# First stage of batches 2 to 7: all 32 columns through the folded transform, from a re-laid-out copy of x

## The chip, the cores and the metric

One NeuronCore of one Trainium2 chip runs the whole program. The metric is device time in microseconds of one execution, the median of several runs; the traces are of one profiled execution.

## What is computed

The program mixes tokens with a global filter in the frequency domain and then applies a two-layer network with SiLU, all in fp32. Cut to what matters:

```
x: 8 x 3008 x 256,  filt_r, filt_i: 1505 x 256,  w_in: 256 x 2048,  w_out: 2048 x 256
y   = irfft(rfft(x, axis=1) * (filt_r + 1j*filt_i), n=3008, axis=1)
h   = y.reshape(24064, 256) @ w_in
out = (h * sigmoid(h)) @ w_out
```

## The kernel before

**The transform.** A sequence of 3008 is split as 94 rows times 32 columns. Stage 1 takes, for each column, a transform over the 94 rows; `forward` takes the transform over the 32 columns; then come the filter's products, `inverse`, and `stage3`, which makes `y`. Between the stages the data goes through DRAM (`d1`, `d2`) to change its layout. Eight batches are treated one after the other.

Stage 1 of batches 2 to 7 uses the symmetry of the cosine and sine tables twice. Rows n and n + 47 are added and subtracted. For columns 0 to 23 (three pieces f = 0, 1, 2 of 8 columns) row n is also paired with its mirror row, which leaves 24 rows to sum over. A folded piece is loaded into `x_all` by `load_fold` (L400), combined on VectorE by `fold` (L412) in four parts k = 0 to 3, multiplied by `stage1_fold` (L427) in sixteen 24-row by 32-column matmuls with 512 columns of data (four column pairs q, each in a quarter of the rows and with a PSUM bank of its own, times four tables k), copied out of PSUM by `evict_fold` (L438), and stored to `d1` from GpSimd's queue (L446). The mirrored rows are prepared in DRAM by `reverse_x` (L388), which copies x in reversed row order. Columns 24 to 31 (pieces u = 6, 7 of 4 columns) are not mirrored: `load_x` (L311) loads them, `sums` (L332) forms sum and difference, `stage1` (L339, matmuls at L354) multiplies with 47 rows and 64 table columns, and `evict_t1` (L381) and L361 copy out.

**The network.** The tokens of a batch are treated in 6 groups (`pairs`), each in 8 steps over the hidden width, so 48 steps per batch (`STEPS`). A step is seven matmuls of `hidden` (L745) and seven of `project` (L804), interleaved in eight rounds; both use a seven-product scheme with 2 x 2 blocks, so VectorE must form sums of PSUM results and of SiLU outputs (helper `combine`, L729) between them. `project` lags `hidden` by one step. Within a step `hidden` writes two PSUM tiles, px (bank "x") and pyz (bank "yz"), each with a single buffer: px is read by ScalarE (copies at L766, L773, L779 and a SiLU at L762), pyz by VectorE. The first pyz matmul of a step waits for the VectorE sum that reads the last pyz of the step before.

**The order.** Nothing is scheduled automatically; each engine executes its instructions in the order in which they are recorded. `put(step, round, piece)` (L619) enters a piece of the spectral work, `until` (L1200) records everything that is due between the rounds. `plan` (L625) enters a batch's pieces at steps relative to `at`, the batch's first step; "step -44" means `at - 44`. `open_step` (L684) enters pieces ahead of a step, after the first two matmuls of `project`; such pieces may use the banks "x" and "yz" (`HIDDEN`, L617) while `hidden` has not yet begun the step. In step -44 the unfolded pieces u = 6 (in the hidden banks) and u = 7 (in the two buffers "f") stand so (L649). Loads and stores of the output are issued from SyncE's queue (SP) in the same order; output tiles are transposed on VectorE (L871) and stored at L882, two of these transposes in step -46 and two in step -45.

For batch 2 the trace has step -46 at 412.21 us, step -45 at 418.25 us and step -44 at 424.30 us, counted from the start of the span.

The functions that the diff touches:

Of the kernel before, what the change touches and what calls it, by code (L numbers as in the profile page):

```python
# [46 lines left out]
FP32 = mybir.dt.float32  # L47
# [23 lines left out]


# [23 lines left out]
def dft_tables():  # L96

    wf = np.zeros((128, 2, 64))
    for par in range(2):
        for i, idx in enumerate(ORDER):  # L100
            ph = 2 * np.pi * (np.arange(N1) * (2 * idx + par) % 94) / 94
            for h in range(2):
                wf[64 * h:64 * h + N1, par, 2 * i] = np.cos(ph)
                wf[64 * h:64 * h + N1, par, 2 * i + 1] = -np.sin(ph)


# [58 lines left out]
    return (wf.astype(f32), wx.reshape(96, 128).astype(f32), wq.astype(f32), wi.astype(f32),  # L165
# [5 lines left out]
def kernel(  # L171
    ctx: ExitStack,
    tc: tile.TileContext,
    x: bass.AP,
    filt_r: bass.AP,
# [8 lines left out]
    wf_host, wx_host, wq_host, wi_host, d_host, e_host = dft_tables()  # L184
    wf_dram = nc.inline_tensor(wf_host, name="wf_tbl")
# [34 lines left out]
    wf_t = cpool.tile([128, 2, 64], FP32)  # L220
# [47 lines left out]
    def spectral(b):  # L268
# [42 lines left out]
        def load_x(u, queue=None):  # L311


            xs[u] = x_t[u % 2]
            if b == 1:
                xs[u] = xs[u].rearrange("p a n -> p (a n)")
                return load_rows(xs[u], u, 1, queue)
            for h in range(2):
                for r0, nr in ((0, 32), (32, N1 - 32)):
                    nc.sync.dma_start(  # L320
                        out=xs[u][64 * h + r0:64 * h + r0 + nr],
                        in_=bass.AP(tensor=x.tensor,
                                    offset=x.offset + (b * S + 32 * r0 + 4 * u + 2 * h) * C,
                                    ap=[[32 * C, nr], [32 * N1 * C, 2], [1, 2 * C]]))
# [7 lines left out]
        def sums(u):  # L332
            ut = x_t[0] if u == 7 else upool.tile([128, 2, 512], FP32, name=f"u_{b}_{u}", tag="u")
            xt = xs.pop(u)
            for par, op in ((0, ALU.add), (1, ALU.subtract)):
                nc.vector.tensor_tensor(out=ut[0:111, par], in0=xt[0:111, 0], in1=xt[0:111, 1], op=op)
            us[u] = ut

        def stage1(u, ahead=True):  # L339
            t1 = tpool.tile([128, 2, 2, C], FP32, name=f"t1_{b}_{u}", tag="t")  # L340
            ps = [bank(b, f"pa_{b}_{u}_{h}", HIDDEN[h] if b > 1 and u == 6 else None) for h in range(2)]
            if b == 1:
                xt = xs.pop(u)
                for h in range(2):
                    nc.tensor.matmul(out=ps[h].rearrange("p n c -> p (n c)"), lhsT=wx_t,  # L345
                                     rhs=xt[0:96, 512 * h:512 * h + 512], start=True, stop=True)
                if ahead and u + 2 < 8:
                    load_x(u + 2)
            else:
                ut = us.pop(u)  # L350
                for par in range(2):
                    for h in range(2):
                        rows = slice(64 * h, 64 * h + N1)
                        nc.tensor.matmul(out=ps[h][64 * par:64 * par + 64], lhsT=wf_t[rows, par],  # L354
                                         rhs=ut[rows, par], start=True, stop=True)
            if b > 1 and u == 7:
                us["t1"] = t1, ps
                return
            for h in range(2):
                copy = nc.scalar.copy if b == 1 or h == 0 else nc.vector.tensor_copy  # L360
                copy(out=t1[:, h], in_=ps[h])  # L361
            if b == 1:
                us["t1", u] = t1
                if ahead:
                    store_rows(u)
                return
            store_t1(u, t1)
# [7 lines left out]
        def store_t1(u, t1):  # L375
            for par in range(2):
                nc.gpsimd.dma_start(
                    out=d1[par].rearrange("s p n c -> (s p) n c")[:, 4 * u:4 * u + 4, :],
                    in_=t1[64 * par:64 * par + 2 * NS].rearrange("p h n c -> p (h n) c"))

        def evict_t1(u, h):  # L381
            t1, ps = us["t1"]
            copy = nc.vector.tensor_copy if h else nc.scalar.copy
            copy(out=t1[:, h], in_=ps[h])
            if h:
                store_t1(u, t1)

        def reverse_x():  # L388

            us["xr"] = dpool.tile([2, 24, 32 * C], FP32, name=f"xr_{b}", tag="xr")  # L390
            at = x.offset + b * S * C
            nc.sync.dma_start(out=us["xr"][:, 1:24],
                              in_=bass.AP(tensor=x.tensor, offset=at + 46 * 32 * C,
                                          ap=[[32 * N1 * C, 2], [-32 * C, 23], [1, 32 * C]]))
            for k in range(2):
                nc.sync.dma_start(out=us["xr"][k, 0:1],
                                  in_=bass.AP(tensor=x.tensor, offset=at + (1 - k) * 32 * N1 * C,
                                              ap=[[32 * C, 1], [1, 32 * C]]))

        def load_fold(f):  # L400

            at = x.offset + (b * S + 8 * f) * C
            for q in range(4):
                rows = slice(32 * q, 32 * q + 24)
                n0 = (8 * f + 2 * q) * C
                nc.sync.dma_start(out=x_all[rows, 0],
                                  in_=bass.AP(tensor=x.tensor, offset=at + 2 * q * C,
                                              ap=[[32 * C, 24], [32 * N1 * C, 2], [1, 2 * C]]))
                nc.sync.dma_start(out=x_all[rows, 1],
                                  in_=us["xr"][:, :, n0:n0 + 2 * C].rearrange("k m n -> m k n"))  # L410
# [16 lines left out]
        def stage1_fold(f):  # L427
            ut = us.pop("f")
            rhs = x_all[:, 0, 0], x_all[:, 1, 0], ut[:, 0], ut[:, 1]
            ps = [bank(b, f"pf_{b}_{f}_{q}", (0, 1, None, None)[q]) for q in range(4)]  # L430
            for k in range(4):
                for q in range(4):
                    rows = slice(32 * q, 32 * q + 24)
                    nc.tensor.matmul(out=ps[q][32 * k:32 * k + 32], lhsT=wq_t[rows, k], rhs=rhs[k][rows],  # L434
                                     start=True, stop=True)
            us["ps"] = ps

        def evict_fold(f, q):  # L438
            if q % 2 == 0:
                us["tf"] = tpool.tile([128, 2, 2, C], FP32, name=f"tf_{b}_{f}_{q}", tag="t")  # L440
            copy = nc.scalar.copy if q < 2 else nc.vector.tensor_copy
            copy(out=us["tf"][:, q % 2], in_=us["ps"][q])  # L442
            if q % 2:
                n0 = 8 * f + 2 * q - 2
                for k in range(4):
                    nc.gpsimd.dma_start(  # L446
                        out=d1[k // 2, :, k % 2, n0:n0 + 4],
                        in_=us["tf"][32 * k:32 * k + NS].rearrange("p q n c -> p (q n) c"))
# [161 lines left out]
        return dict(us=us, store_rows=store_rows, evict_y=evict_y, evict_t1=evict_t1, halves=halves, load_first=load_first, stage1_first=stage1_first, fill_first=fill_first, load_x=load_x, load_two=load_two, sums=sums, stage1=stage1, reverse_x=reverse_x,  # L610
# [8 lines left out]
    def put(step, rnd, piece, *args):  # L619

        pending.append((step + rnd / ROUNDS, len(pending), lambda: piece(*args)))
# [3 lines left out]
    def plan(b, part):  # L625
# [6 lines left out]
        else:  # L632
            put(at - 72, 0, part["reverse_x"])
            for f, step, load, places in ((0, -56, -66, ((-60, 3), (-60, 5), (-59, 5), (-58, 5))),
                                          (1, -48, -55, ((-52, 3), (-52, 5), (-51, 5), (-50, 5))),
                                          (2, -40, -44, ((-42, 5), (-41, 3), (-41, 5), (-40, 3)))):
# [3 lines left out]

                put(at + step, 7, part["stage1_fold"], f)
# [4 lines left out]
            for u, step in ((6, -46), (7, -45)):  # L646
                put(at - 47, 0, part["load_x"], u)
                put(at + step, 5, part["sums"], u)
            open_step(at - 44, (part["stage1"], 6), (part["stage1"], 7))  # L649
            put(at - 44, 3, part["evict_t1"], 7, 0)  # L650
            put(at - 44, 5, part["evict_t1"], 7, 1)
# [515 lines left out]
    for t, dram in ((wf_t, wf_dram), (wq_t, wq_dram)):  # L1167
        put(20, 0, lambda t=t, dram=dram: nc.sync.dma_start(out=t, in_=dram.ap()))
# [56 lines left out]
_INS = ['x', 'filt_r', 'filt_i', 'moe_w_in', 'moe_w_out']  # L1225
# [26 lines left out]
```

## Time and profile before

| what | value |
|---|---|
| time, 3 runs | median 2576.61 us (2576.21 to 2581.67) |
| span of the profiled execution, first to last instruction | 2574.2 us |
| TensorE clock granted, mean | 0.997 |
| L354, unfolded stage 1, matmul records | 96, 589 to 615 ns each |
| L434, folded stage 1, matmul records | 576, 600 ns each |
| L425, fold, 1024 columns / 512 columns | 1.22 us / 0.68 us |
| L336, sums, 512 columns | 0.68 us |
| L442, a bank copied out, ACT / DVE | 0.59 us / 0.68 us |
| DMA over the span | 66 GB/s, 171.08 MB |

No end-to-end time is recorded for the profiled execution beside its span; the span is 2.4 us below the median of the three runs. An fp32 matmul appears as two records. Records of small tiles overlap in time, so a block's length is read from the start of its first record to the start of the next block. PE is TensorE, PEld its weight loads, DVE VectorE, ACT ScalarE, POOL GpSimd, SP SyncE.

### The profile page before, as it was taken

What the parts mean: (1) busy time and instruction counts of PE and PEld (TensorE: products, weight loads), DVE (VectorE), ACT (ScalarE), POOL (GpSimd) and SP (SyncE); (2) the same over time, 40 slices, a digit from 0 to 9 for tenths busy, and PEclk for the clock granted to TensorE, in tenths of its full rate; (3) what the DMA queues carried; (4) which work ended last, traced back from release to release, by engine and by line L of the source; (5) the groups of instructions that cost most, each with busy time, mean ns of one, the idle gap of its engine ahead of it and who ended that gap; (6) DMA issues with size and microseconds to landing.
All of it is one profiled execution on the core that took longest, in us unless ns stands there. A gap on an engine that the chain in (4) does not pass through costs nothing.

```text
span 2574.2 us, 48031 instructions
## 1 busy us (share of the span) xinstructions
PE 2550.8 (99%) x18810; PEld 2195.8 (85%) x18810; DVE 1665.8 (65%) x3591; ACT 1086.3 (42%) x3009; POOL 429.1 (17%) x685
## 2 busy tenths in 40 slices
PE   8999999999999999999999999999999999999998
PEld 6688888888888888888888888888888888888987
DVE  7866666676666666666666676666666666555554
ACT  3544444444444444444444444444444444444443
POOL 3212111211121111311121111211121112101101
PEclk9999999999999999999999999999999999999999
DMA  9522232222222222322223122331232211200011
GB/s 290 160 60 53 78 70 64 60 73 67 59 64 68 73 67 50 82 70 67 58 73 78 48 67 63 76 79 46 66 85 67 67 42 33 60 18 16 9 17 17
DMA packets 199611, 171.08 MB, mean 66 GB/s; under 512 B 122068, under 2 KB 173380, under 8 KB 198500
## 3 DMA queue, kind: packets, MB, share of 16 engines
q1 hardware_dynamic: 178392, 117.06, 19.7%
q0 software_dynamic: 17344, 45.70, 5.6%
q10 hardware_dynamic: 3648, 5.24, 0.7%
q8 instruction: 148, 2.42, 0.4%
q14 instruction: 79, 0.65, 0.1%
HBM read 96.07 MB, written 81.26 MB: 69 GB/s over the span
## 4 chain that ended last, share of the span: by engine, by line
PE 96%; DMA 1%; DVE 1%; issue 0%; ACT 0%; POOL 0%; SPq 0%; DVEq 0%; ACTq 0%
PE acc L821 44%; PE px L758 26%; PE pyz L758 19%; PE pd L588 2%; PE pb L467 2%; PE pc L510 2%; PE pf L434 1%; PE pc L530 0%; DMA filt<-in_filt_i_dram 0%; PE pa L354 0%; DMA w_t<-in_x_dram 0%; PE pa L345 0%; DMA d_t<-d_tbl 0%; DVE w_t L988 0%; DMA raw<-in_moe_w_in_dram 0%
## 5 line engine op out<-in xcount | busy, mean ns | idle before, releaser
L821 PE MATMUL acc<-g,w_t 128*128 128x256 f32 (+1 forms) x5376 | 1510.2, 375 | 0.4 <-DVE g L729 0.4
L821 PEld LDWEIGHTS acc<-g,w_t 128*128 128x128 f32 x5376 | 1023.0, 190 | 114.4 <-DVE g L729 0.8
L729 DVE TENSOR_TENSOR g<-pyz,abc 128x256 f32<-128x256 f32 (+1 forms) x1152 | 480.1, 417 | 620.1 <-ACT abc L779 356.6
L729 DVE TENSOR_TENSOR g<-g 128x256 f32<-128x256 f32 (+3 forms) x1152 | 599.7, 521 | 196.7 <-ACT g L762 183.5
L758 PE MATMUL px<-ty,w_t 128*128 128x256 f32 (+1 forms) x2304 | 679.1, 376 | 1.8 <-ACT abc L773 1.2
L762 ACT ACTIVATE g<-g 128x256 f32<-128x256 f32 (+1 forms) x1152 | 472.9, 411 | 250.7 <-DVE g L729 250.7
L729 POOL TENSOR_TENSOR s<-s 128x256 f32<-128x256 f32 (+1 forms) x329 | 254.9, 792 | 1417.8 <-DVE s L841 1289.7
L758 PEld LDWEIGHTS px<-ty,w_t 128*128 128x128 f32 x2304 | 432.7, 190 | 65.3 <-issue 6.2
L758 PE MATMUL pyz<-y,w_t 128*128 128x256 f32 (+1 forms) x1536 | 454.1, 377 | 0.0
L758 PEld LDWEIGHTS pyz<-y,w_t 128*128 128x128 f32 x1536 | 283.8, 190 | 47.6 <-DVE g L729 7.7
L773 ACT COPY abc<-px 128x256 f32<-128x256 f32 (+1 forms) x384 | 141.2, 368 | 372.7 <-PE px L758 372.7
L779 ACT COPY abc<-px 128x256 f32<-128x256 f32 (+1 forms) x384 | 141.5, 368 | 338.1 <-PE px L758 337.1
L762 ACT ACTIVATE g<-px 128x256 f32<-128x256 f32 (+1 forms) x384 | 145.8, 380 | 300.9 <-PE px L758 300.7
L758 PE MATMUL px<-y,w_t 128*128 128x256 f32 (+1 forms) x768 | 232.3, 384 | 1.0 <-DVE y L602 1.0
L758 PE MATMUL pyz<-ty,w_t 128*128 128x256 f32 (+1 forms) x768 | 225.4, 375 | 0.2 <-DVE g L729 0.2
L758 PEld LDWEIGHTS px<-y,w_t 128*128 128x128 f32 x768 | 140.5, 190 | 32.9 <-DVE y L608 5.8
L758 PEld LDWEIGHTS pyz<-ty,w_t 128*128 128x128 f32 x768 | 144.5, 190 | 18.7 <-DVE g L729 1.0
L766 ACT COPY abc<-px 128x256 f32<-128x256 f32 (+1 forms) x384 | 135.3, 352 | 52.3 <-PE px L758 52.3
L588 PEld LDWEIGHTS pd<-wi_t,t 48*64 48x64 f32 x3840 | 61.2, 135 | 25.3 <-ACT g L762 16.4
L446 POOL DMA_DIRECT2D d<-tf x144 | 71.6, 504 | 29.5 <-DVE tf L442 29.5
L871 DVE STREAM_TRANSPOSE o<-s 128x256 f32<-128x256 f32 x192 | 74.0, 423 | 0.4 <-issue 0.4
L841 ACT COPY s<-acc 128x512 f32<-128x512 f32 (+1 forms) x94 | 54.2, 577 | 47.6 <-PE acc L821 47.3
(137 smaller groups left out, 1264.4 us busy)
## 6 DMA issues: line engine op xcount, KB each, us to landing
t<-d SPq DMA_DIRECT2D x120, 192.0 KB
t<-d SPq DMA_DIRECT2D x84, 256.0 KB
d<-q POOLq DMA_DIRECT2D x84, 256.0 KB, 2.7
out_dram<-o SPq DMA_DIRECT2D x636, 32.0 KB
d<-tf POOLq DMA_DIRECT2D x144, 96.0 KB, 3.5
xr<-in_x_dram SPq DMA_DIRECT2D x6, 1472.0 KB
x_all<-in_x_dram SPq DMA_DIRECT2D x72, 96.0 KB
x_all<-xr SPq DMA_DIRECT2D x72, 96.0 KB
```

The lines of the kernel that those rows point to most:

```text
L446: nc.gpsimd.dma_start(out=d1[k // 2, :, k % 2, n0:n0 + 4], in_=us["tf"][32 * k:32 * k + NS].rearrange("p q n c -> p (q n) c"))
L467: nc.tensor.matmul(out=ps[k][32 * j:32 * j + 32, ri, :], lhsT=d_t[rows, 4 * g + at, ri, :], rhs=rhs, start=True, stop=True)
L588: nc.tensor.matmul(out=ps[h][c0:c0 + 64, cb, i, :], lhsT=t4[rows, i, 128 * cb + c0:128 * cb + c0 + 64], rhs=wi_t[rows, :], start=True, sto ...
L729: eng.tensor_tensor(out=out, in0=in0, in1=in1, op=op)
L758: nc.tensor.matmul(out=out, lhsT=w_t[:, jp, c, 0], rhs=rhs, start=start, stop=True, skip_group_check=True)
L762: nc.scalar.activation(out=g[:, k, 0:n], in_=g[:, k, 0:n] if src is None else src, func=AFT.Silu)
L766: nc.scalar.copy(out=sums[:, 0, 0:n], in_=xo)
L773: nc.scalar.copy(out=sums[:, 1, 0:n], in_=xo)
L779: nc.scalar.copy(out=sums[:, 2, 0:n], in_=xo)
L821: nc.tensor.matmul(out=acc[pair][i][:, h, 0:n], lhsT=w_t[:, jp, c, 1], rhs=g[:, k, 0:n], start=(jp == 0 and h == 0), stop=last, skip_group ...
L841: copy(out=s[:, 2 * i:2 * i + 2, 0:n], in_=acc[pair][i][:, :, 0:n])
L871: v.transpose(out=o[:, :, h, :], in_=results[pair][:, ((2, 6), (4, 1))[chunk][h], :])
```

## The change

The input x of batches 2 to 7 is also handed over as `folded`, an array laid out in numpy before the launch: for each batch and each of four pieces a block of 128 partitions by 2048 words that holds the rows, the mirrored rows and zeros in the unused partitions. It is a rearrangement; no arithmetic is done. `load_fold` becomes one DMA of a whole block (1 MB). `reverse_x`, the unfolded pieces (`load_x`, `sums`, the 47-row matmuls, `evict_t1`, `store_t1`) and the table `wf` are gone for these batches. A fourth folded piece, f = 3, takes columns 24 to 31. It is loaded at step -47, folded in steps -46 and -45, and multiplied in the open step -44, with q = 0 and 1 in the hidden banks "x" and "yz". Batches 0 and 1 are as before.

```diff
+def folded_rows(x):
+    rows = np.asarray(x)[2:].reshape(B - 2, 2, N1, 4, 4, 2 * C)
+    out = np.zeros((B - 2, 4, 4, 32, 2, 2, 2 * C), rows.dtype)
+    for k in range(2):
+        out[:, :, :, 0:24, 0, k] = rows[:, k, 0:24].transpose(0, 2, 3, 1, 4)
+        out[:, :, :, 1:24, 1, k] = rows[:, k, 46:23:-1].transpose(0, 2, 3, 1, 4)
+        out[:, :, :, 0, 1, k] = rows[:, 1 - k, 0]
+    return out.reshape(B - 2, 4, 128, 8 * C)
...
         def load_fold(f):
-            at = x.offset + (b * S + 8 * f) * C
-            for q in range(4):
-                rows = slice(32 * q, 32 * q + 24)
-                n0 = (8 * f + 2 * q) * C
-                nc.sync.dma_start(out=x_all[rows, 0], ...)
-                nc.sync.dma_start(out=x_all[rows, 1], in_=us["xr"]...)
+            nc.sync.dma_start(out=x_all.rearrange("p i a n -> p (i a n)"), in_=folded[b - 2, f])
...
         def stage1_fold(f):
-            ps = [bank(b, f"pf_{b}_{f}_{q}", (0, 1, None, None)[q]) for q in range(4)]
+            home = (*HIDDEN, None, None) if f == 3 else (0, 1, None, None)
+            ps = [bank(b, f"pf_{b}_{f}_{q}", home[q]) for q in range(4)]
...
         def evict_fold(f, q):
-            copy = nc.scalar.copy if q < 2 else nc.vector.tensor_copy
+            copy = nc.scalar.copy if (q % 2 == 0 if f == 3 else q < 2) else nc.vector.tensor_copy
...
-            put(at - 72, 0, part["reverse_x"])
             for f, step, load, places in ((0, -56, -66, ((-60, 3), (-60, 5), (-59, 5), (-58, 5))),
                                           (1, -48, -55, ((-52, 3), (-52, 5), (-51, 5), (-50, 5))),
+                                          (3, -44, -47, ((-46, 3), (-46, 5), (-45, 3), (-45, 5))),
                                           (2, -40, -44, ((-42, 5), (-41, 3), (-41, 5), (-40, 3)))):
...
+                if f == 3:
+                    open_step(at + step, (part["stage1_fold"], f), (part["evict_fold"], f, 0),
+                              (part["evict_fold"], f, 1))
+                    put(at + step, 3, part["evict_fold"], f, 2)
+                    put(at + step, 5, part["evict_fold"], f, 3)
+                    continue
...
-            for u, step in ((6, -46), (7, -45)):
-                put(at - 47, 0, part["load_x"], u)
-                put(at + step, 5, part["sums"], u)
-            open_step(at - 44, (part["stage1"], 6), (part["stage1"], 7))
-            put(at - 44, 3, part["evict_t1"], 7, 0)
-            put(at - 44, 5, part["evict_t1"], 7, 1)
```

## The prediction

> **What bounds the kernel now.** I read the page first: the busy table, the clock row, the chain.
>
> ```profile
> PE 2550.8 (99%) x18810; PEld 2195.8 (85%) x18810; DVE 1665.8 (65%) x3591; ACT 1086.3 (42%) x3009; POOL 429.1 (17%) x685
> ...
> PEclk9999999999999999999999999999999999999999
> ...
> PE 96%; DMA 1%; DVE 1%; issue 0%; ACT 0%; POOL 0%; SPq 0%; DVEq 0%; ACTq 0%
> ```
>
> TensorE is busy 99% of the span at full clock and is 96% of the chain. A change can pay only by shortening what TensorE does, and can cost only by making TensorE wait. So I went to the timelines of the one stretch that is rewritten, step -44 of batch 2, first on PE:
>
> ```profile
> 424.30 1.03 PE L821 MATMUL acc<-g,w_t 128*128 128x256 f32 x4
> 425.25 1.09 PE L354 MATMUL pa<-u,wf_t 47*64 47x512 f32 x8
> 426.17 1.04 PE L354 MATMUL pa<-x_all,wf_t 47*64 47x512 f32 x8
> 427.13 0.70 PE L758 MATMUL px<-y,w_t 128*128 128x256 f32 x2
> ```
>
> The columns are start, duration, engine, line. The unfolded stage 1 (two pieces, u = 6 and 7) holds TensorE from 425.25 to 427.13: **1.88 us**. The other five batches show the same figure to 0.01 us. Then ACT in that stretch:
>
> ```profile
> 426.39 0.59 ACT L361 COPY t<-pa 128x512 f32<-128x512 f32 x1 [1.02 <-PE pa L354]
> 427.87 0.37 ACT L766 COPY abc<-px 128x256 f32<-128x256 f32 x1 [0.89 <-PE px L758]
> ```
>
> The px matmul at 427.13 writes the bank "x" that this ACT copy empties, and the copy ends at 426.98. It runs beside u = 7's matmuls, so it is nearly hidden. Now a folded piece (f = 1, same batch), PE and ACT:
>
> ```profile
> 403.90 0.66 PE L434 MATMUL pf<-x_all,wq_t 24*32 24x512 f32 x8
> ...
> 404.97 1.17 PE L588 MATMUL pd<-wi_t,t 48*64 48x47 f32 x64
> ```
>
> ```profile
> 405.18 1.07 ACT L442 COPY tf<-pf 128x512 f32<-128x512 f32 x2 [0.29 <-PE pf L434]
> ```
>
> Its sixteen matmuls run side by side and hold TensorE for 404.97 - 403.90 = **1.07 us**, but the first eviction starts 1.28 after the first matmul, since all four banks fill together. There pd fills TensorE meanwhile, in other banks.
>
> **Part 1: TensorE, and the new wait.** Per batch, 1.88 us of matmuls go and 1.07 come. If the next matmul could follow at once, that is -0.81 us, six batches -4.9 us. But in the changed order px stands right behind the new piece, and bank "x" is the new piece's q = 0 bank. So: piece starts at T = 425.25, ACT copy starts T + 1.28, takes 0.59 (L442), ends T + 1.87. TensorE idles for the last 0.8 of this. Queued behind that px are all matmuls of the step. The lag from a copy's end to the released weight load has two rows. At the start of step -45 a g<-pyz ends at 418.46 + 0.42 = 418.88, and the pyz load that waits for it starts 0.05 later:
>
> ```profile
> 418.93 0.38 PEld L758 LDWEIGHTS pyz<-y,w_t 128*128 128x128 f32 x2
> ```
>
> At the old piece it is 427.13 - 426.98 = 0.15, but there TensorE was not free before 426.17 + 0.92 = 427.09 anyway (u = 6 occupied 0.92). I take 0.05: px starts at T + 1.92 instead of T + 1.88, **+0.04 per batch, +0.2 us in all**; with 0.15 it is +0.14, +0.8 in all. The other hidden bank, "yz", is emptied by DVE in parallel: T + 1.28 + 0.68 (L442 on DVE) + 0.05 = T + 2.01, and pyz follows px by 0.54, so it does not wait. The evictions of q = 2 and 3 stand where those of u = 7 stood, with the same lengths (0.59 and 0.68).
>
> The Trainium skill weighs in here: "TensorEngine Tiling", "Performance Considerations", says that finer tiling speeds up TensorE and not the emptying of PSUM, which may then be the bottleneck. By tile counts alone the sum would be -4.9 us; by this rule nothing is left of it; the rows above give +0.2.
>
> **Part 2: DVE.** Four subtractions and additions of 512 columns (L336) go from steps -46 and -45; a fold comes: two operations of 1024 columns (1.22 us, L425) in step -46, four of 512 (0.68) in step -45, at rounds 3 and 5. The rows now:
>
> ```profile
> 415.12 0.77 DVE L871 STREAM_TRANSPOSE o<-s 128x256 f32<-128x256 f32 x2
> 416.70 0.42 DVE L729 TENSOR_TENSOR g<-pyz,abc 128x256 f32<-128x256 f32 x1 [0.82 <-ACT abc L779]
> 417.04 1.28 DVE L336 TENSOR_TENSOR u<-x_all 111x512 f32<-111x512 f32 x2
> 418.46 0.42 DVE L729 TENSOR_TENSOR g<-pyz,abc 128x256 f32<-128x256 f32 x1
> ...
> 421.10 0.76 DVE L871 STREAM_TRANSPOSE o<-s 128x256 f32<-128x256 f32 x2
> 422.75 0.42 DVE L729 TENSOR_TENSOR g<-pyz,abc 128x256 f32<-128x256 f32 x1 [0.88 <-ACT abc L779]
> 423.09 1.28 DVE L336 TENSOR_TENSOR x_all<-x_all 111x512 f32<-111x512 f32 x2
> 424.50 0.42 DVE L729 TENSOR_TENSOR g<-pyz,abc 128x256 f32<-128x256 f32 x1
> ```
>
> The second g<-pyz of a step has no slack: the next pyz load starts 0.05 after it ends. Two 0.68 operations take 1.28 together, so successors overlap by 0.08. Step -46: transposes end 415.89, the first fold operation starts 415.81, its successor 415.81 + 1.14 = 416.95 (g<-pyz 0.25 late, which only delays a SiLU that ACT reaches later anyway); then 0.34 on, the second at 417.29, and the tight g<-pyz can start at 418.43, before its 418.46. Step -45: transposes end 421.86; 421.78 + 1.20 = 422.98, then 423.32 + 1.20 = 424.52 instead of 424.50; it ends 424.94, before T. **Cost nothing**, with 0.03 to spare. Without any overlap: step -46 415.89 + 1.22 + 0.42 + 1.22 = 418.75, 0.29 late; step -45 421.86 + 1.37 + 0.42 + 1.37 + 0.42 = 425.44, so TensorE would start at 425.49, 0.24 late; 0.53 per batch, +3.2 us. A gain is excluded, since nothing waits for the old sums. I take the overlapped value: it is this stage's own row.
>
> The skill's "VectorE: DVE Perf Modes", in the section on the TRN2 errata, times an fp32 tensor_tensor at (N + 151) / 0.96 ns, 1.22 us and 0.69 us here, which the rows' durations confirm. Charged in full per operation it is about the case without overlap, +3.2 us; the rows' spacing says nothing.
>
> **Part 3: DMA.** SP's issues per batch fall from 3 + 24 + 8 = 35 to 4, and the device-side reversal (L392, L396) goes; SP stood still for it from 249 to 280 us, stores queued behind it, yet TensorE's steps there that hold no spectral piece keep their 6.04 us, so freeing SP is worth nothing. POOL issues 8 stores in place of 4 (0.5 us each), 15 us or more before the last piece's stores, on a queue idle for 13 us before them. The one new deadline: x_all for the new piece is loaded by one DMA of 1.05 MB at about 407.1 (where L320's eight now begin), in place of 0.75 MB, and the fold reads it at 415.81. In 406.06 to 412.21 the DMA moved 196 GB/s. With the 0.39 MB of t<-d ahead of it the load needs (1.05 + 0.39) / 0.196 = 7.3 us from 406.2, done at 413.5, 2.3 us early. If the d<-tf stores from 409.13 (0.79 MB) all went ahead too: 11.4 us, 417.6, 1.8 us late. I take no wait, because 8 KB rows in place of 2 KB runs need fewer packets.
>
> **Sum.** 0.2 + 0 + 0. The profiled execution's span is 2574.2 us, 2.4 below the median of 2576.61; I carry these 2.4 along: 2574.2 + 0.2 + 2.4 = **2576.8 us**. Measurement of this kernel tells about 0.2% from no change: below 2571.5 or above 2581.8.
>
> **Rivals.**
> - The saved TensorE time shows (px not held by the eviction): 2576.6 - 4.9 = 2571.7. For it: the block shrinks from 1.88 to 1.07. Against: one bank, one copy, in order.
> - DVE does not overlap, or each fold operation waits a little: 2576.6 + 0.2 + 3.2 = 2580.0, and 2580.6 with the longer lag. For it: only 0.03 us of slack. Against: the spacing rows.
> - Slower for good: x_all lands late. Place: the fold's first operation in step -46; DVE then holds the tight g<-pyz and TensorE stops with it. It decides from 415.81 on, and every microsecond after it costs 6 us; at 417.6 it is 10.7 us, 2587.5; at one microsecond 2582.8.
> - The change does not do what it says: the instruction order of the changed program has 16 folded matmuls per batch in that place and no L354; excluded.
>
> **How the numbers follow.** Forecast 0.80 (own range 2575.5 to 2578.5); saving shows in part or whole 0.07 (0.03 below 2571.5); DVE overrun 0.08 (0.02 above 2581.8); late landing 0.05 (nearly all above). Faster 0.03, slower 0.07, same 0.90. The range takes in the forecast, the bounds of lag and fold, and part of the saving: 2574.0 to 2580.6.
>
> **What would show it.** In step -44: sixteen matmuls starting 425.25 and px about 1.92 later, with the wait put down to ACT tf, and PE idle about 0.8 us before it. In steps -46 and -45: periods of 6.04 us as now. If these steps lengthen, part 2 or 3 was wrong: DVE idle before the first fold operation means the load, none means the queue. If px follows after 1.1 us, part 1 was.

## The result, and the profile after

The changed kernel took 2581.28 us (median of 21 runs, 2577.18 to 2583.51); the kernel before, on the same chip and in turn with it, 2577.33 us (21 runs, 2574.25 to 2583.03). The ratio is **1.0014, 95% interval 1.0008 to 1.0020**: 2.1 to 5.2 us slower, 3.3 us between the means (2581.12 and 2577.85). No change had been forecast, 2576.8 us with a range up to 2580.6. The profiled execution of the kernel after took 2580.56 us, its span 2578.5 us.

In the listing, a line number of the kernel after is 63 below the one that the kernel before has for the same statement (L758 is now L695, L821 is L758, L442 is L379, L425 is L361 with one line more). The page of the kernel after, two of the rows shown for before (the clock row is unchanged):

```profile
PE 2547.5 (99%) x18906; PEld 2193.4 (85%) x18906; DVE 1677.5 (65%) x3603; ACT 1086.1 (42%) x3009; POOL 440.0 (17%) x709
...
PE 96%; DMA 1%; DVE 1%; issue 0%; ACT 0%; ACTq 0%; POOL 0%; SPq 0%; DVEq 0%
```

TensorE is busy 3.3 us less and the span is 4.3 us longer. The page's shares don't tell why. So the rewritten stretch comes next, step -44 of batch 2, on PE (start, duration, engine, line):

```profile
426.03 1.03 PE L758 MATMUL acc<-g,w_t 128*128 128x256 f32 x4
426.99 0.66 PE L371 MATMUL pf<-x_all,wq_t 24*32 24x512 f32 x8
...
428.93 0.70 PE L695 MATMUL px<-y,w_t 128*128 128x256 f32 x2 [0.80 <-ACT tf L379]
```

and on ACT:

```profile
428.29 0.58 ACT L379 COPY tf<-pf 128x512 f32<-128x512 f32 x1 [1.17 <-PE pf L371]
```

The folded piece starts at T = 426.99, the copy of bank "x" at T + 1.30; the copy ends at T + 1.88, and px starts at T + 1.94. The unfolded pieces held TensorE for 1.88. The wait is put down to this copy, 0.80 us, and it comes in all six batches; in the list of PE's waits it is 4.8 us, six times. DVE in steps -46 and -45:

```profile
417.54 1.18 DVE L361 TENSOR_TENSOR uf<-x_all 120x1024 f32<-120x1024 f32 x1
418.64 0.41 DVE L666 TENSOR_TENSOR g<-pyz,abc 128x256 f32<-128x256 f32 x1
418.98 1.21 DVE L361 TENSOR_TENSOR x_all<-x_all 120x1024 f32<-120x1024 f32 x1
420.19 0.42 DVE L666 TENSOR_TENSOR g<-pyz,abc 128x256 f32<-128x256 f32 x1
...
425.06 1.28 DVE L361 TENSOR_TENSOR uf<-x_all 120x512 f32<-120x512 f32 x2
426.26 0.41 DVE L666 TENSOR_TENSOR g<-pyz,abc 128x256 f32<-128x256 f32 x1
```

The fold fits between the sums, with no idle time ahead of it: the load was there (issued at 408.8, and these loads land 5.6 us after issue in the median). The two steps keep 6.04 and 6.05 us. So far the forecast holds. What is left is outside this stretch. The instructions with which the engines close the program have a line of their own (L1247 before, L1184 after); the views of engine work leave them out, the view of that one line shows them. Among them every engine has some called DRAIN. Kernel before, the last matmuls (start, duration) and GpSimd's DRAINs (engine's sequencer, operation, count: shortest/median/longest in ns, first and last start in us):

```profile
2563.23 1.89 PE L821 MATMUL acc<-g,w_t 128*128 128x240 f32 x8 [0.41 <-DVE g L729]
...
L1247 POOLq DRAIN  x3: 46/102/5640, 2567.8 to 2574.0; - x3
```

Kernel after:

```profile
2565.52 1.89 PE L758 MATMUL acc<-g,w_t 128*128 128x240 f32 x8 [0.41 <-DVE g L666]
...
L1184 POOLq DRAIN  x3: 46/102/7593, 2570.1 to 2578.2; - x3
```

GpSimd's first DRAIN here starts in both kernels 2.70 us after the end of TensorE's last matmul (2565.12 and 2567.40, the ends of the matmul rows above), right behind GpSimd's last two stores. Before it takes 5.64 us, after **7.59 us**. SP is through with its own part of the end some 7.6 us after the last matmul (its first DRAIN, 7 ns long, stands at 2572.7 before and 2574.9 after), and what follows on SP comes only after GpSimd's DRAIN. From the last matmul to the end of the span it is 9.12 us before and 11.08 us after, **+1.96 us**. GpSimd issues 302 DMAs before and 326 after.

One more row differs, PE's waits inside the 128 records of a pd block in step 40 of batch 3:

```profile
1294.79 2.06 PE L525 MATMUL pd<-wi_t,t 48*64 48x47 f32 x122
...
1297.64 0.33 PE L525 MATMUL pd<-wi_t,t 48*64 48x47 f32 x6 [0.79 <-issue]
```

Before, the block at this place is one piece:

```profile
1292.86 2.10 PE L588 MATMUL pd<-wi_t,t 48*64 48x47 f32 x128
```

TensorE stops for 0.79 us and nothing that the profile shows ends the wait. Steps were compared one by one, from the first px of a step to the first px of the next, counted from 0 in each batch; step 3 then holds the folded piece of the next batch. From step 8 of the first batch to the last matmul, the kernel after has +0.06 six times (the folded piece), +1.08 and +0.27 in the step 40 of batches 3 and 0, -0.35 in that of batch 4, -0.26 and -0.28 in two steps of batches 6 and 7, and no other difference over 0.04 us: +0.83 in all. The start, up to step 8, took 137.8 us before and 139.3 us after in these two executions; the experiments show between 136.2 and 142.4 us whatever the kernel, and it goes largely with the time for which the clock stood at a half there (6.8 us in the two shortest starts, 17.1 us in the two longest; 10.2 and 13.7 us in these two executions), so it counts as chance.

### The profile page after: what moved, and what is told of

Same layout as the page of the kernel before. It is cut to its first block, busy times and chain, and to the rows that moved or that the text cites. A ratio compares the mean times of both kernels' runs of the same rounds, so it can differ in the third digit from the quotient of the medians.

```text
span 2578.5 us, 48042 instructions
## 1 busy us (share of the span) xinstructions
PE 2547.5 (99%) x18906; PEld 2193.4 (85%) x18906; DVE 1677.5 (65%) x3603; ACT 1086.1 (42%) x3009; POOL 440.0 (17%) x709
## 3 DMA queue, kind: packets, MB, share of 16 engines
q0 software_dynamic: 18112, 45.70, 5.4%
## 4 chain that ended last, share of the span: by engine, by line
PE 96%; DMA 1%; DVE 1%; issue 0%; ACT 0%; ACTq 0%; POOL 0%; SPq 0%; DVEq 0%
PE acc L758 44%; PE px L695 26%; PE pyz L695 19%; PE pd L525 2%; PE pb L404 2%; PE pc L447 2%; PE pf L371 1%; PE pc L467 1%; DMA w_t<-in_x_dram 0%; PE pa L328 0%; DMA filt<-in_filt_r_dram 0%; DMA d_t<-d_tbl 0%; DVE w_t L925 0%; DMA t<-d 0%; DMA raw<-in_moe_w_in_dram 0%
## 5 line engine op out<-in xcount | busy, mean ns | idle before, releaser
L758 PE MATMUL acc<-g,w_t 128*128 128x256 f32 (+1 forms) x5376 | 1509.4, 375 | 0.4 <-DVE g L666 0.4
L758 PEld LDWEIGHTS acc<-g,w_t 128*128 128x128 f32 x5376 | 1021.6, 190 | 115.8 <-DVE g L666 0.8
L695 PE MATMUL px<-ty,w_t 128*128 128x256 f32 (+1 forms) x2304 | 678.4, 376 | 1.5 <-ACT abc L710 1.1
L695 PEld LDWEIGHTS px<-ty,w_t 128*128 128x128 f32 x2304 | 432.3, 190 | 65.0 <-issue 6.2
L695 PE MATMUL pyz<-y,w_t 128*128 128x256 f32 (+1 forms) x1536 | 454.3, 377 | 0.4 <-DVE g L666 0.4
L695 PEld LDWEIGHTS pyz<-y,w_t 128*128 128x128 f32 x1536 | 283.8, 190 | 48.2 <-DVE g L666 7.8
L695 PE MATMUL px<-y,w_t 128*128 128x256 f32 (+1 forms) x768 | 232.7, 385 | 6.0 <-ACT tf L379 4.8
L695 PE MATMUL pyz<-ty,w_t 128*128 128x256 f32 (+1 forms) x768 | 225.3, 375 | 0.2 <-DVE g L666 0.2
L695 PEld LDWEIGHTS px<-y,w_t 128*128 128x128 f32 x768 | 140.6, 190 | 38.6 <-ACT tf L379 10.3
L695 PEld LDWEIGHTS pyz<-ty,w_t 128*128 128x128 f32 x768 | 144.4, 190 | 18.9 <-DVE g L666 1.0
L383 POOL DMA_DIRECT2D d<-tf x192 | 95.0, 501 | 127.1 <-DVE tf L379 69.2
```

What stands on the lines that cost most here:

```text
L383: nc.gpsimd.dma_start(out=d1[k // 2, :, k % 2, n0:n0 + 4], in_=us["tf"][32 * k:32 * k + NS].rearrange("p q n c -> p (q n) c"))
L695: nc.tensor.matmul(out=out, lhsT=w_t[:, jp, c, 0], rhs=rhs, start=start, stop=True, skip_group_check=True)
L758: nc.tensor.matmul(out=acc[pair][i][:, h, 0:n], lhsT=w_t[:, jp, c, 1], rhs=g[:, k, 0:n], start=(jp == 0 and h == 0), stop=last, skip_group ...
```

## The experiments

Theory: the change is slower because GpSimd issues more DMAs, which lengthens its DRAIN at the end; the folded piece adds 0.4 us. Rivals: the fold or its load (the rivals of the prediction), the array from numpy, or the wait for bank "x".

**Take the added stores off GpSimd** (kernel after):

```diff
-                    nc.gpsimd.dma_start(
+                    (nc.sync if f == 3 else nc.gpsimd).dma_start(
```

> The changed kernel with one edit: the eight stores of the fourth folded piece (f = 3) are issued from SyncE's queue in place of GpSimd's, so GpSimd issues 278 DMAs in place of 326 (before: 302). Theory: of the about 3.6 us that the changed kernel is slower, 2.0 are the last DRAIN of GpSimd, which took 5.64 us with 302 DMAs and 7.59 with 326, and so grows 0.08 us per DMA issued there. Then the DRAIN here is about 3.7 us, it no longer ends last, and the time is 2.5 to 2.9 us below the changed kernel's, about 2578.6, ratio 1.0005. Rival: the DRAIN's length has nothing to do with the number of DMAs and the loss comes from the start of the kernel and the loads; then it stays between 5.6 and 7.6 and the ratio stays near 1.0014.

2578.12 us, ratio to before 1.0005 (0.9996 to 1.0014). GpSimd issues 278 DMAs, the DRAIN takes 4.27 us, and the end after the last matmul is 8.36 us. The +0.06 stays in five of the six steps; that of batch 3 has +0.24. It is now SP that ends last, so a shorter DRAIN would bring nothing more.

**Add the stores to the kernel before**, with everything else as it was: each store of its unfolded pieces becomes two of half the rows, the same bytes.

```diff
-                nc.gpsimd.dma_start(
-                    out=d1[par].rearrange("s p n c -> (s p) n c")[:, 4 * u:4 * u + 4, :], ...
+                for r in (0, NS):
+                    nc.gpsimd.dma_start(
+                        out=d1[par].rearrange("s p n c -> (s p) n c")[r:r + NS, 4 * u:4 * u + 4, :], ...
```

> The kernel before with one edit: each of the four stores per batch of the unfolded pieces (L377) is split into two of 24 partitions, so GpSimd issues 326 DMAs as in the changed kernel; bytes and descriptor sizes of the data are the same, nothing else is changed. Theory: the last DRAIN of GpSimd takes 7.6 us and the time rises by 2.0 us, ratio 1.0008. Rival (the DRAIN follows bytes, or chance): 5.6 us and ratio 1.0000.

326 DMAs, DRAIN 7.61 us, end 11.08 us, as in the kernel after, without any of its other edits:

```profile
L1248 POOLq DRAIN  x3: 46/102/7608, 2568.7 to 2576.8; - x3
```

So the number of DMAs makes the long end, not the bytes. The time, 2578.06 us, ratio 1.0004 (0.9995 to 1.0012), is unclear by itself: 2 us is 0.0008.

**Cover the wait for bank "x"** (kernel after): one of the two early project matmuls of step -44 is recorded behind the folded piece.

```diff
-            for _ in range(2):
+            for _ in range(1 if step in between else 2):
                 next(work[1])
         until(step - 0.05)
+        if step in between:
+            next(work[1])
```

> The changed kernel with one edit: in step -44 one of the two project matmuls that stand ahead of the fourth folded piece is moved behind it, between the piece and the px matmul that waits for the eviction. Theory: px is held by ACT's copy of bank x, about 1.9 us after the piece's first matmul, and TensorE idles 0.8 us there; with the move the piece starts about 0.28 earlier (when the last reader of bank yz is done), the moved matmul fills 0.43 of the gap, and the two steps together get about 0.28 us shorter per batch, 1.7 us in all, about 2579.6, ratio 1.0008. Rival: px is not held by the eviction but by the change of tiling; then the gap stays 0.8 and the time that of the changed kernel, ratio 1.0014.

2580.41 us, ratio 1.0007 (0.9998 to 1.0016). The trace answers better than the time: each of the six steps is 0.20 us shorter than before (0.26 shorter than after; 0.28 was expected), the DRAIN is still 7.61 us. The wait for the copy is real, and covering it doesn't touch the end.

**The loads alone** (kernel before, with the array and one DMA for pieces 0 to 2, no mirrored copy in DRAM; pieces u = 6 and 7 unfolded):

```diff
-            for q in range(4):
-                ...
+            nc.sync.dma_start(out=x_all.rearrange("p i a n -> p (i a n)"), in_=folded[b - 2, f])
...
-            put(at - 72, 0, part["reverse_x"])
```

> The kernel before with one part of the change alone: pieces f = 0 to 2 are loaded by one DMA each from the re-laid-out array, the reversal in DRAM is gone, and the unfolded pieces stay as they were. GpSimd issues 302 DMAs. Theory: no step and no DRAIN changes, ratio 1.0000, within 0.7 us of the kernel before. Rival: the further input, its place in memory or the large loads cost time at the start or in the steps; then 1 to 4 us slower.

2578.47 us, ratio 1.0001 (0.9992 to 1.0011); DRAIN 5.64 us with 302 DMAs, end 9.13 us, steps as before but for +0.27 and +0.06 us in two steps 40. The array from numpy shows no effect on the time, as far as this measurement tells (0.001).

**The fold alone** (kernel after with the loads of before: mirrored copy and eight small DMAs per piece, for four pieces):

> The kernel after without the array from numpy: the mirrored rows are copied in DRAM and each of the four pieces is loaded by eight small DMAs, as before; the fourth piece stays folded, its stores stay on GpSimd. If the fold alone makes the whole change (GpSimd issues 326 DMAs): last DRAIN on POOL 7.6 us, tail after the last matmul 11.1 us, step 3 of batches 1 to 6 +0.06 us each, ratio to before 1.0012 or so. If the array from numpy has a part in it: the tail or the steps stand between those of before and after. Eight more small loads per batch stand on SP ahead of the load of the fold; if they land late, steps 1 and 2 of a batch are longer.

2580.36 us, ratio 1.0012 (1.0003 to 1.0021). DRAIN 7.59 us, end 11.08 us: the long end comes with the fold and its stores, not with the loads. The expected +0.06 per batch was missed: it is +0.24 to +0.42, and step 2 of batch 3 has +1.07, where DVE waited 1.29 us for the last small load. So the one-DMA load, without effect on the old kernel, keeps these steps at +0.06 here; only the one in batch 3 is traced to a late load.

**All stores of folded pieces on SP** (kernel after, `nc.sync` for all f):

> The kernel after with all stores of folded pieces issued from SP, so GpSimd issues 134 DMAs. If the last DRAIN goes with the count: below the 4.27 us of 278 DMAs (the slopes so far, 0.057 and 0.082 us per DMA, would bring it to zero or to a floor of its own), and the tail no shorter than 8.36 us, where SP ends its own work at 7.6 us. If the drain is set by something else near the end of the program, it stays above 4 us. The stores on SP wait for evictions, and loads queue behind them: if that matters, single steps lengthen by tenths of a us; if not, the steps are those of after.

2581.51 us, ratio 1.0020 (1.0011 to 1.0029). With 134 DMAs the DRAIN is 3.28 us and the end 8.37 us, but the load of the fourth piece now queues on SP behind stores that wait for copies. DVE, batch 3:

```profile
1046.94 1.23 DVE L361 TENSOR_TENSOR uf<-x_all 120x1024 f32<-120x1024 f32 x1 [2.75 <-DMA x_all<-in_folded_dram]
```

This is the late landing of the prediction's third rival, in a kernel where it really happens: 2.75 us of waiting lengthens that step by 2.53 us; four of the six batches have it, 6.2 us in all.

**Both repairs** (one project matmul behind the piece, the fourth piece's stores on SP):

> Both repairs together: the kernel after, with the second project matmul of step -44 recorded behind the folded piece, and the stores of the fourth piece on SP. If both terms add: step 3 of a batch -0.20 us against before (six times, -1.2), tail 8.36 us (-0.76), the pd stalls in step 40 about +0.5 as in the other runs of this order; in all about -1.5 us against before, ratio 0.9994, and 0.998 against after. If the stores on SP cost what they bring, the ratio is 1.000 or more.

2576.78 us, ratio 0.9995 (0.9987 to 1.0004). DRAIN 4.28 us, end 8.31 us, five of the six steps -0.20 us, that of batch 3 +0.04. Both terms are in the trace, the first in five of six steps.

**More DMAs still** (kernel after, each store of the fourth piece issued as two):

```diff
+                    if f == 3:
+                        for h in range(2):
+                            nc.gpsimd.dma_start(out=d1[k // 2, :, k % 2, n0 + 2 * h:n0 + 2 * h + 2],
+                                                in_=us["tf"][32 * k:32 * k + NS, h])
+                        continue
```

> The kernel after with each store of the fourth piece issued as two of half the columns: the same bytes, 374 DMAs on GpSimd in place of 326. If the end goes with the count at 0.06 to 0.1 us per DMA: last DRAIN 10.5 to 12.5 us, tail 14 to 16 us, 3 to 5 us more than after, ratio to before about 1.003. If the drain depends on bytes or on the last few transfers: 7.6 us and the ratio of after, 1.0014.

2577.68 us, ratio 1.0003 (0.9994 to 1.0012). Here the theory in its first form **fell**: with 374 DMAs the DRAIN takes 3.29 us, not 10.5 to 12.5. It does not simply grow with the number. Three kernels for the shape, one execution each, by the same edit for half of the fourth piece (350), for f = 2 and 3 (422) and for all f (518):

> The kernel after, with one of the two groups of stores of the fourth piece split in two: 350 DMAs on GpSimd, between 326 (DRAIN 7.6 us) and 374 (3.3 us). If the DRAIN is a sawtooth over the number of DMAs with its fall between 326 and 374: either 9.5 to 10 us (rising still) or 3.3 us (past the fall). A value between 4 and 7 us would mean that the number does not set it.

> The stores of the third and fourth piece split: 422 DMAs on GpSimd. If a sawtooth restarts between 326 and 374, 422 is at most 96 past it and the DRAIN is at its floor of 3.3 us or little above (4.3 us at most). If 374 was low for another reason, it rises above 7.6 us.

> All stores of folded pieces split: 518 DMAs on GpSimd, 240 above the 278 of the run with the stores of the fourth piece on SP. If a sawtooth of a period near 240 to 350 holds: about 4 us. If the DRAIN only goes with how late GpSimd's last DMAs are, 3.3 us. Rising above 7.6 us would speak for plain growth with the number.

The DRAIN took 9.56, 5.55 and 4.17 us, the end 13.04, 9.13 and 8.32 us. With the runs above, and the one that follows, the counts fall on one curve when taken modulo 120:

| DMAs on GpSimd | modulo 120 | DRAIN, us |
|---|---|---|
| 134, 374 | 14 | 3.28, 3.29 |
| 278, 518 | 38 | 4.27, 4.17 |
| 302 (before), 422 | 62 | 5.64, 5.55 |
| 326 (after, and the kernel before with split stores) | 86 | 7.59, 7.61 |
| 350, 470 | 110 | 9.56, 9.47 |

The count of 470 was chosen to test this. With the stores of f = 1, 2 and 3 split, 470 DMAs:

> The stores of three of the four pieces split: 470 DMAs on GpSimd. The nine counts so far fit a DRAIN that depends on the count modulo 120 (302 and 422: 5.64, 5.55 us; 278 and 518: 4.27, 4.17; 134 and 374: 3.28, 3.29). 470 is 110 modulo 120, as 350 is, which took 9.56: the DRAIN should take 9.4 to 9.6 us and the tail 13.0. Any value below 6 or above 11 us would break the law.

9.47 us, end 13.05 us: the law held at a count that was not used to find it. Packets don't explain it: from 302 to 326 DMAs those on GpSimd's queue rise by 768 (17344 to 18112), from 326 to 350 by 384 (to 18496), and the DRAIN by 1.96 us both times. All the counts in the table lie 24 apart, so where between 110 and 134 the DRAIN falls is not shown. Two rows, of the kernels with 350 and with 374 DMAs:

```profile
L1190 POOLq DRAIN  x3: 46/102/9557, 2569.9 to 2579.9; - x3
```

```profile
L1190 POOLq DRAIN  x3: 46/102/3293, 2573.7 to 2579.1; - x3
```

**Let the DRAIN run early** (kernel after): GpSimd's two stores of the last output tile go to SP and ACT.

```diff
-                    turn = (0, 1, rr, 2) if chunk == 0 else (0, 1, 0, 1)
+                    turn = (0, 1, rr, 1 - rr) if chunk == 0 else (0, 1, 0, 1)
```

> The kernel after, with GpSimd's two stores of the last output tile issued from SP and ACT (four on each in place of three); GpSimd issues 324 DMAs, the last of them long before the end. If the DRAIN is work that GpSimd can do as soon as it has nothing left, it starts some 26 us before the last matmul, whatever it takes, and the tail goes back from 11.08 to 8.4 us, plus up to 0.6 us for the store that SP and ACT have more: -2.1 to -2.7 us against after, ratio to before 1.0004. If GpSimd can't drain before the other engines end, or the drain is set by these last two stores, the tail stays near 11 us or the DRAIN falls to its 3.3 us in the same place.

2577.55 us, ratio 0.9999 (0.9990 to 1.0008). The DRAIN still takes 7.01 us, with 324 DMAs, but at another time:

```profile
L1184 POOLq DRAIN  x3: 46/102/7012, 2539.8 to 2574.5; - x3
```

It starts at 2539.8, 26.6 us ahead of the last matmul, and is over before the other engines end; the end is 8.42 us, -2.66. So the DRAIN lengthens the end only where it is the last thing to run; the end waited for it, not for the stores as such. The control, the kernel before with the same edit:

> The kernel before with GpSimd's two last stores issued from SP and ACT, the control of last_stores_off_pool. If the DRAIN then lies ahead of the end, the tail falls from 9.12 to 8.42 us as in that run, -0.7 us; the kernels before and after, both with this edit, then differ by what is left of the change, +0.4 to +0.8 us, where they differed by 3.3 us in the mean. If the gain in last_stores_off_pool came from something else in that kernel, the tail here stays at 9.1 us.

2577.29 us, ratio 0.9998 (0.9989 to 1.0006); DRAIN 5.05 us with 300 DMAs, early as well; end 8.73 us, -0.39 where -0.7 was expected. With the DRAIN out of the way the kernels of before and after stand at 0.9998 and 0.9999 of the kernel before, where they were 0.0014 apart; each of the two ratios is uncertain by 0.0009, or 2 us, so this alone tells little of what is left. The two early DRAINs, with 300 and 324 DMAs, differ by 1.96 us as well, but lie some 0.4 us below the line of the table.

**The change with its wait covered and its end cleared**, with one project matmul behind the piece, and with two (a third one is then taken early, and `project` rests in one round more):

> The kernel after with the order acc, pf, acc, px in step -44 and GpSimd's two last stores on SP and ACT. If both terms add: step 3 of a batch -0.20 us against before, six times -1.2; tail 8.42 (-0.7); the pd stalls 0 to +0.5, the fixed -0.54 of two steps of batches 6 and 7: in all about -1.5 to -2 us against before, ratio 0.9993.

> As between_last_stores_off_pool, with one more project matmul between the folded piece and px: acc, pf, acc, acc, px. The idle time of TensorE ahead of px, 0.4 us with one acc there, should be filled: step 3 of a batch -0.55 to -0.60 us against before (the full saving would be -0.81), six times -3.4; tail 8.42; in all -4 us against before, ratio 0.9985. If the later px delays ACT's copies and the sums of the step, the step keeps -0.20 or the next one gets longer by as much.

With one: 2576.48 us, ratio 0.9996 (0.9988 to 1.0005), six times -0.21, end 8.33 us. With two: **2574.60 us, ratio 0.9987 (0.9978 to 0.9996)**, the only version whose interval against the kernel before lies below 1. Its step -44, batch 2:

```profile
426.10 0.60 PE L759 MATMUL acc<-g,w_t 128*128 128x256 f32 x2
426.62 0.83 PE L371 MATMUL pf<-x_all,wq_t 24*32 24x512 f32 x8
...
427.88 1.13 PE L759 MATMUL acc<-g,w_t 128*128 128x256 f32 x4
428.85 0.60 PE L696 MATMUL px<-y,w_t 128*128 128x256 f32 x2
```

PE has no idle time ahead of px any more. Yet a batch gains 0.33 us, not the expected 0.55 to 0.60: a step later one px starts 0.19 us late, at 432.49, after ACT's copies; the copy of the third bank (431.36, 0.58 us) now stands ahead of the one that this px waits for.

**The kernel after, once more:**

> The kernel after, unchanged, once more. The terms found so far that repeat are +1.96 us (end), +0.37 us (six times 0.06 at the folded piece) and +0.29 us (end-to-end time beyond the span: 2.08 against 1.79 us), 2.6 us together, ratio 1.0010; the first 21 runs had +3.3 us in the mean at a mean granted clock of 0.9956 against 0.9965 of before. If the clock was chance, this run shows 0.9965 and a ratio near 1.0010; if the change lowers the clock, 0.9956 again and 1.0013. In the trace: last DRAIN 7.6 us, step 3 +0.06 us; the stalls of step 40 (pd) and the start may fall elsewhere.

2581.06 us, ratio 1.0014 (1.0005 to 1.0023), clock 0.9958. The trace repeats: DRAIN 7.60 us, six times +0.06, step 40 of batch 3 +1.35.

## Why the prediction was wrong

**Failed step: Part 3, the stores on GpSimd, with the last sentence of the Sum.** The prediction priced "POOL issues 8 stores in place of 4" at nothing, because they lie 15 us ahead of the piece's last stores, on a queue that is idle there. At that place it was right. But it looked for the price only there. The Sum carried the whole span over but for the 0.2 us, and so took the end of the program as fixed; the trace of before showed 9.1 us from the last matmul to the end of the span, 5.64 of them GpSimd's DRAIN, and the step asked neither what that DRAIN consists of nor whether 24 more DMAs touch it. The runs put +1.96 us there: the kernel before with 24 more DMAs has it, the fold alone has it, the loads alone have not, and with the DRAIN moved away from the end it is gone. None of the rivals was this one. A part of the distance is not the change at all: the forecast of 2576.8 was built on a median of three runs, 2576.61, and 21 runs of the same kernel give 2577.33, so 0.7 of the 4.5 us between forecast and result lie in the base.

**Part 1 was right in mechanism and small in size.** The saved matmuls were eaten by the wait for the copy of bank "x", as forecast: 0.80 us idle. Per batch it is +0.06 in place of +0.04: first matmul to copy 1.30 for 1.28, copy to px 0.06 for 0.05, six times +0.37 us in place of +0.2. The Trainium skill's rule from "TensorEngine Tiling", "Performance Considerations", that emptying PSUM may become the bottleneck, agrees with this case (0.80 us of waiting in each batch). The -4.9 us of the first rival were never to be had: with the wait covered by other matmuls, px comes 2.75 us after the acc ahead of the piece, with three pairs of acc (0.43 us each) in between; the piece costs 2.75 - 1.29 = 1.46 us there. Read as the 1.07 ahead of pd was read, from its start to the start of the next block, it is 427.88 - 426.62 = 1.26; the rest lies in the acc before and behind it. The unfolded pieces, counted in the same way, cost 427.13 - 424.30 - 2 x 0.43 = 1.97, so by this estimate about 0.5 per batch is the limit, and 0.33 was reached.

**Part 2 was right.** The fold operations overlap their successors by 0.08, and the steps kept their length. The measured time, 2581.28, lies beside the 2580.0 to 2580.6 of the rival "DVE does not overlap". The trace excludes it all the same: a number that fits isn't a cause.

**Part 3, the load, was right:** no wait. Its bound was real, as the two kernels with late loads show.

**Not in the prediction's terms:** the stalls of pd and two shorter steps. In nine traces with the folded piece and the order of the kernel after, step 8 to the last matmul took 2427.7 to 2428.8 us, 0.89 more in the mean than the trace of before (2427.3; the four traces with the order of the kernel before lie between 2426.9 and 2427.6); 0.37 of it is the folded piece and 0.5 is this. The two shorter steps are in the kernel before with split stores as well, so the fold doesn't make them. The start, up to step 8, is left out of the sum: it is 139.3 us in the mean of the nine traces and 138.4 in the mean of the four, with a spread of 3 us and more, so a difference can't be told from chance. The end-to-end time exceeds the span by 1.79 us before and 2.08 after (the 2.4 of the prediction set a span against the median of three runs). The sum of what was found is 1.96 + 0.37 + 0.5 + 0.3 = 3.1 of the 3.3 and, in the repeat, 3.6 us between the means.

**Still open:** what GpSimd does in the DRAIN and why the period is 120; what stops TensorE inside a pd block; the 0.3 us beyond the span, which other kernels have or lack without a pattern that I could see; and a small rest in the clock. The kernel after ran at a mean granted clock of 0.9956 and 0.9958, the kernel before at 0.9964 in its 123 runs beside the experiments. But this mean covers the whole span, and in all the traces the clock stands at a half from 2 to 5 us after the last matmul on, where TensorE has nothing to do: for 5.6 us before and 8.2 us after, which alone makes 0.0005 between these two traces. The 0.0003 or less that is left would be half a microsecond, since over all runs 0.001 of clock goes with 1.6 us; the runs can't tell it from chance.

## What to carry to other kernels

Price an added DMA also at the end of the program: read what comes after the last matmul, which engine is last there, and move that engine's last work so that its closing work runs under others. A wait that eats a saving shows in the engine's idle row; other work recorded between the producer and the waiting instruction gets part of it back, as far as the next wait allows. When the forecast effect is 0.01% and the result 0.14%, step-by-step differences of two traces find a cause that medians can't.

## What the runs showed of the hardware

- GpSimd's first DRAIN at the end takes 3.3 to 9.6 us by the number of DMAs that GpSimd issued, modulo 120; it repeats to 0.02 us for the same count and to 0.1 us for counts 120 or 240 apart. Between 62 and 110 it is 0.08 us per DMA. Splitting stores, the same bytes in more DMAs, moved it by +2 us or by -4.3 us. The Trainium skill, "VectorE: DVE Perf Modes", "The DRAIN you can't avoid", speaks of short constant DRAINs, about 12 ns, from the code around a program on all engines. No run here shows whether it means those on the kernel's last line; of these SP's take 7 ns, GpSimd's first one doesn't fit, and the measurement decides.
- The sixteen matmuls of a folded piece take 1.07 us of TensorE ahead of pd, and 1.26 us between project matmuls of 128 rows, both from start to start.
- Executions of one kernel differ by up to 11 us (2572 to 2583 for the kernel before), mostly with the granted clock, 0.999 to 0.994. In the traces the clock falls to a half within the first 90 us, for 3.4 us or a multiple of that, at places that differ from one execution to the next (before: 3.4 us each at 15.5, 53.0 and 80.3 us; after: 6.8 us at 51.3, 3.4 us at 75.2 and 82.0 us), and once more after the last matmul.
